# Position-bias stage: high parts of the weight split on ScalarE, low parts and refilling loads one chunk later, three buffers for the mirrored copies

## Chip, core and metric

One Trainium2 chip, one core. The metric is the device time of one execution in microseconds (us), median of three runs. Engine names are those of the profile: PE is TensorE (PEld its weight loads), DVE is VectorE, ACT is ScalarE, POOL is GpSimd, SP is the engine that issues most DMAs ("SPq" rows).

## What is computed

Attention with a learned position bias, a gated dense layer, and a routed mixture of experts:

```python
psi_rel = np.log1p(np.abs(pos[:, None] - pos[None, :]))
x = (psi_rel / psi_i)[..., None]
bias = np.maximum(x @ w1 + b1, 0.0) @ w2            # one bias matrix per head, 576 x 576
scores = q @ k.T / np.sqrt(D) + bias                # 4 batches, 8 heads
x = softmax(scores) @ v                             # 2304 tokens x 512
x = ((x @ m_w1) * (x @ m_w2) @ w3) @ w_out          # dense layer
out = routed_experts(x)                             # 8 experts, one per token
```

The dense layer's last two matrices are multiplied with each other ahead of time (w3 times w_out). That product, and the position bias, are the work of the first stage of the kernel, the function `p0`. The change touches this stage alone.

## The kernel before

**Two jobs in one stage.** `p0` runs two jobs side by side. The first builds the position bias in nine groups (gg = 0 to 8) of 3 to 5 row tiles t. For each group 16 masks are made, nine on ACT and seven on DVE (line 262 on DVE, line 260 on ACT). For each tile of a group PE runs 48 small matmuls on the masks (line 341) into one of three PSUM buffers `pb`; `evac` then scales one half on ACT (line 267, `tmp`) and adds both halves on DVE (line 278, `ds`). A tile's evacuation is written one tile later than its matmuls. After every second group `flush` sends each `ds` tile to DRAM (`dsym`, line 220), and where the tile has a mirrored half POOL copies it in reverse, four heads at a time, into a buffer `md` (line 234), which a DMA writes to `dsym` too (line 237). There are two `md` buffers; a copy waits until the DMA of the copy two before it has read its buffer.

**The second job.** w_out and w3 arrive as raw 64-bit numbers in 24 chunks c of 128 x 512 (8 of w_out, then 16 of w3, two for each block f), over five raw buffers. A chunk is converted to float32 by one ACT step (line 88, done a whole chunk ahead by `begin`) and three DVE steps (lines 90, 91, 92). It is then split for TensorE: the high part is a rounded copy (line 201, on POOL), the low part is the difference of the number and its high part (line 206, on DVE). Where the low part is written, the refilling load of the chunk five further on is put into SP's queue (line 179). When both parts are there, `wp_mm` multiplies (line 244, three matmuls for each of 64 steps, 48 of them in this stage and 16 in the next); after eight steps ACT copies the result into a buffer of the same `md` ring (line 248) and SP sends it off (line 249, `wp`).

**The order.** Engines take their instructions in the order in which the program writes them. Within a tile that order is: the `wp_mm` steps that `WPH` gives to the tile, the tile's 48 matmuls, the ACT half of the previous tile's evacuation, two or three ACT masks, a slice of the list `mixed`, the DVE half of the evacuation with its flush, and the tasks of `ahead` (from group 3 on: the loads of q, k and v of the first head at the second tile of group 3, and from the fourth tile on the steps that split them, the first of which is an ACT copy of q, line 402). `mixed` holds the DVE masks of the next group, the placing of the coefficients (line 160), and the conversion steps, sorted by a due time between 0 and 1. A group converts `CONV[gg+1] - CONV[gg]` chunks. For chunk number x of a group of n chunks the three DVE steps are due at (x + 0.125)/n, (x + 0.375)/n and (x + 0.625)/n, the high part at (x + 0.75)/n, and the low part with the load at (x + 1.25)/n but at the end of the group at the latest. For the last chunk of every group, so, the low part stands right behind the high part.

POOL's other work in this stage is the mirrored copies, the coefficients of a later group (lines 151, 153, 165) and some of the steps that split q, k and v.

Of the kernel before, what the change touches and what calls it, by code (L numbers as in the profile page):

```python
# [9 lines left out]
F32 = mybir.dt.float32  # L10
# [5 lines left out]
ALU = mybir.AluOpType  # L16
# [4 lines left out]
B, H, S, D = 4, 8, 576, 64  # L21
HID = 32
NT = B * S
DM = 512
FF = 1024
E = 8
P = 128
# [15 lines left out]

CV = [(i, b) for i in range(12) for b in range(2)]
CONV = (0, 5, 9, 11, 13, 16, 17, 20, 22, 24)
WPH = (0, 0, 0, 2, 12, 16, 31, 32, 43, 48)

NACT = 9

FM = 0.6  # L50
NRAW = 5


LAG = 6
# [15 lines left out]
class Kern:  # L70
# [4 lines left out]
    def T(self, pool, shape, dt, tag, **k):  # L75
        self.n += 1
        return pool.tile(shape, dt, name=f"{tag}_{self.n}", tag=tag, **k)
# [18 lines left out]
    def p0(self, dsym, wp_dram, late, ahead=lambda gg, ti: None):  # L96


        nc, tc, I, T = self.nc, self.tc, self.I, self.T
        with ExitStack() as es:  # L100
# [3 lines left out]
            st = es.enter_context(tc.tile_pool(name="p0s", bufs=2, side="right"))  # L104
# [37 lines left out]
            gp = nc.gpsimd  # L142
# [32 lines left out]
            def load(i, b):  # L175
                raws[i, b] = T(st, [P, DM, 2], I32, "w3", bufs=NRAW)
                src = I["w_out"][:, 2 * i:2 * i + 2, :] if i < 4 else I["w3t"][i - 4]
                src = src.rearrange("p k d -> p (k d)")[:, DM * b:DM * b + DM]
                nc.sync.dma_start(out=raws[i, b].rearrange("p n t -> p (n t)"), in_=src.bitcast(I32))
# [3 lines left out]
            def begin(n):  # L183
                if n < len(CV):
                    i, b = CV[n]
                    t_, steps = self.conv_steps(st, raws.pop((i, b)), "w3t", bufs=4)
                    steps[0]()
                    begun[i, b] = t_, steps[1:]

            def conv(i, b):  # L190

                t_, steps = begun.pop((i, b))
                if i < 4:
                    hi, lo = (w[:, 2 * i + b, :] for w in (woh, wol))
                else:
                    if b == 0:
                        w3hl[i - 4] = [T(late.wp, [P, KF, P], F32R, n, bufs=2) for n in ("w3h", "w3l")]
                    hi, lo = (w.rearrange("p k f -> p (k f)")[:, DM * b:DM * b + DM] for w in w3hl[i - 4])

                def part():  # L200
                    gp.tensor_scalar(out=hi, in0=t_, scalar1=1.0, scalar2=1.0, op0=ALU.mult, op1=ALU.mult)

                def rest():
                    if order:
                        load(*order.pop(0))
                    v.tensor_tensor(out=lo, in0=t_, in1=hi.bitcast(F32), op=ALU.subtract)

                return steps + [part, rest]
# [3 lines left out]
            def flush(t, kk, d):  # L212
                n = 64 if t == 4 else P
                w = min(128, DMAX[t] - 128 * kk)
                sg = -1 if t >= 2 else 1
                if sg > 0:
                    c0 = OFF[t] + 128 * kk
                else:
                    c0 = OFF[t] - 128 * kk - w + 1
                nc.sync.dma_start(out=dsym[:, t, 0:n, c0:c0 + w].rearrange("h p w -> p h w"), in_=d[:n, :, 0:w])  # L220
                other = OFF[t] if t < 2 else 702 - OFF[t]
                m = min(128 * kk + w - 1, other)
                d0 = max(128 * kk, 1)
                if m < d0:
                    return
                if sg > 0:
                    c1, c2 = OFF[t] - m, OFF[t] - d0 + 1
                    l1 = w - 1 - (m - 128 * kk)
                else:
                    c1, c2 = OFF[t] + d0, OFF[t] + m + 1  # L230
                    l1 = d0 - 128 * kk
                for h in range(0, H, 4):
                    md = T(st, [P, 4, 128], F32, "md")
                    gp.tensor_scalar(
                        out=md[:n, :, 0:w], in0=bass.AP(d.tensor, d.offset + 128 * h + w - 1, [[d.ap[0][0], n], [128, 4], [-1, w]]),
                        scalar1=1.0, scalar2=1.0, op0=ALU.mult, op1=ALU.mult)
                    nc.sync.dma_start(out=dsym[h:h + 4, t, 0:n, c1:c2].rearrange("h p w -> p h w"), in_=md[:n, :, l1:l1 + c2 - c1])

            def wp_mm(f, k, pools=(ps1, st)):
                if k == 0:  # L240
                    pws[f] = T(pools[0], [P, DM], F32, "pv")
                hi, lo = w3hl[f]
                for j, (a, b_) in enumerate(((hi, woh), (hi, wol), (lo, woh))):
                    nc.tensor.matmul(out=pws[f], lhsT=a[:, k, :], rhs=b_[:, k, :],  # L244
                                     start=(k == 0 and j == 0), stop=(k == KF - 1 and j == 2))
                if k == KF - 1:
                    wsb = T(pools[1], [P, DM], F32, "md") if pools[1] is st else T(pools[1], [P, S], F32, "t")[:, 0:DM]
                    nc.scalar.copy(out=wsb, in_=pws.pop(f))
                    nc.sync.dma_start(out=wp_dram[:, f, :], in_=wsb)

# [32 lines left out]
            order = list(CV)  # L283
            for _ in range(NRAW):
                load(*order.pop(0))
# [10 lines left out]
                    pl()  # L296
            pl = coefs(1)
            prev = None
            for gg in range(9):
                ts = [t for t in (0, 4, 3, 1, 2) if 64 * gg < DMAX[t]]  # L300
                wph = list(range(WPH[gg], WPH[gg + 1]))
                bg, bga = [], []
                if gg < 8:
                    for q in range(16):
                        act = (q + 1) * NACT // 16 > q * NACT // 16
                        (bga if act else bg).append(lambda q=q, act=act: mask(gg + 1, q, act))

                cs = []
                n = CONV[gg + 1] - CONV[gg]
                for x, (i, b) in enumerate(CV[CONV[gg]:CONV[gg + 1]]):  # L310

                    cs += [((x + (k + 0.5) / 4) / n, (i, b, k)) for k in range(3)]
                    cs += [((x + 0.75) / n, (i, b, 3)), (min((x + 1.25) / n, 1), (i, b, 4))]
                st_ = {}

                def cstep(i, b, k):
                    if k == 0:
                        begin(CV.index((i, b)) + 1)
                        st_[i, b] = conv(i, b)
                    st_[i, b][k]()  # L320

                items = [(FM * (k + 0.5) / len(bg), x) for k, x in enumerate(bg)]
                items += [(k, lambda x=x: cstep(*x)) for k, x in cs]
                if gg < 8:
                    items.append((0, pl))
                    if gg == 0:
                        items.append((0, lambda: place(1, 1, c3)))
                    if gg < 7:
                        pl = coefs(gg + 2)
                mixed = [x for _, x in sorted(items, key=lambda x: x[0])]  # L330
                nt = len(ts)
                for ti, t in enumerate(ts):
                    for x in wph[len(wph) * ti // nt:len(wph) * (ti + 1) // nt]:
                        wp_mm(x // KF, x % KF)
                    n = 64 if t == 4 else P
                    pb = T(ps, [P, 2, 2, H, 8, 4], F32, "pb")
                    mv = mvs[gg % 2]
                    for s in range(16):
                        m_ = mss[gg, s // 8]
                        for k in range(3):  # L340
                            nc.tensor.matmul(out=pb[:n, s // 8, :, :, s % 8], lhsT=m_[:, s % 8, P * t:P * t + n], rhs=mv[:, k, s], start=(k == 0), stop=(k == 2))  # L341
                    fin = evac(*prev) if prev else None
                    for x in bga[len(bga) * ti // (nt - 1):len(bga) * (ti + 1) // (nt - 1)]:
                        x()
                    m0, m1 = len(mixed) * ti // nt, len(mixed) * (ti + 1) // nt
                    for x in mixed[m0:m1]:
                        x()
                    if fin:
                        fin()
                    ahead(gg, ti)  # L350
                    prev = (gg, t, pb)
            evac(*prev)()
            return [lambda pools, x=x: wp_mm(x // KF, x % KF, pools) for x in range(WPH[9], KF * KF)]


# [1183 lines left out]
```

## Time and profile before

| | us |
|---|---|
| median of 3 runs (lowest, highest) | 1094.40 (1093.64, 1094.58) |
| the profiled execution | 1096.77 |
| span of its trace | 1094.9 |

The profiled execution's span is 1094.9 us, and 1.9 us lie around it; the execution itself was 2.4 us longer than the median. The stage `p0` takes the first 168 us of the span: its last `ds` row ends there and the score matmuls of the attention (line 480) begin. In the trace the groups begin, by their first row of line 160, at 37.2 (group 1), 57.7 (2), 76.3 (3), 97.4 (4), 119.9 (5), 134.8 (6) and 149.9 us (7).

A row of a timeline gives start and duration in us, then engine, line, operation, tiles, and in brackets how long the engine stood idle before it and what it waited for. The row of a wait gives the waiting engine and line, what it waited for, the sum in us, how many times, and the longest. Times in the prediction are us from the span's start.

### The profile page before, as it was taken

The page shows a single profiled execution, that of the slowest core. Times are in us where ns is not written, and L with a number is a line of the kernel's source. Part 1 is how long each engine was busy: PE and PEld are TensorE (multiplying, and loading weights), DVE is VectorE, ACT ScalarE, POOL GpSimd, SP SyncE. Part 2 cuts the span into 40 slices and gives each one's busy share as a digit, 9 for nine tenths or more (in the row PEclk, how much of TensorE's full clock was granted, in tenths as well). Part 3 has the DMA queues.
Part 4 walks back from the last instruction along what each step waited for, and adds up shares of the span by engine and source line. Part 5 has one row for each costly group of instructions (what it writes and reads, how often), then busy time and mean ns, then how long its engine had stood idle before and what let it go on. Part 6 is the DMA issues. An engine that isn't in the chain of part 4 may idle for free.

```text
span 1094.9 us, 21996 instructions
## 1 busy us (share of the span) xinstructions
PE 1009.9 (92%) x8118; PEld 903.7 (83%) x8118; DVE 795.1 (73%) x1490; ACT 668.2 (61%) x1248; POOL 403.5 (37%) x475
## 2 busy tenths in 40 slices
PE   3575887999999999989999999999979999999995
PEld 3565776888888888869999999999978888888884
DVE  8875997899999999999722212221478899989995
ACT  5555465888898988844322222222125888888884
POOL 3443625787888878544400000000043112111120
PEclk9788898999999999989999999999989999999998
DMA  4579677333534341234110000000233316411272
GB/s 133 144 211 227 170 202 206 120 113 109 166 114 131 103 148 56 65 125 141 63 39 1 20 20 20 11 11 20 95 108 111 129 49 212 171 40 39 67 252 94
DMA packets 62419, 116.54 MB, mean 106 GB/s; under 512 B 14495, under 2 KB 33567, under 8 KB 62048
## 3 DMA queue, kind: packets, MB, share of 16 engines
q1 hardware_dynamic: 58496, 104.14, 31.0%
q0 software_dynamic: 3520, 10.75, 2.9%
q8 instruction: 67, 1.10, 0.4%
q14 instruction: 48, 0.39, 0.1%
q10 hardware_dynamic: 288, 0.15, 0.1%
HBM read 155.68 MB, written 25.15 MB: 165 GB/s over the span
## 4 chain that ended last, share of the span: by engine, by line
PE 49%; issue 15%; DMA 11%; DVE 7%; ACT 1%; POOL 0%; POOLq 0%; DVEq 0%; ACTq 0%
PE ab L711 16%; DMA out<-or,sci 9%; PE sc L480 8%; PE o L780 8%; PE pv L566 6%; PE tr L517 5%; PE pv L561 3%; DMA raw<-in_w 2%; PE pv L510 1%; PE pv L244 1%; DVE cva L91 1%; DVE cva L90 1%; DVE cva L89 1%; DVE cva L92 1%; DVE su L501 0%
## 5 line engine op out<-in xcount | busy, mean ns | idle before, releaser
L506 POOL TENSOR_SCALAR e<-e,su 128x576 f32<-128x576 f32 x144 | 114.9, 801 | 58.7 <-DVE su L502 45.0
L757 DVE TENSOR_TENSOR g<-ab,asb 128x256 f32<-128x256 f32 x72 | 30.4, 422 | 143.3 <-ACT asb L756 143.0
L341 PE MATMUL pb<-mv,mask 128*128 128x64 bf16 (+1 forms) x1872 | 73.6, 206 | 53.0 <-DVE ds L278 40.1
L341 PEld LDWEIGHTS <-mask 128*128 128x128 bf16 (+1 forms) x1872 | 70.0, 111 | 61.1 <-issue 53.1
L487 DVE CUSTOM_DVE_ANT_0 t<-sc,nb 128x576 f32<-128x576 f32 x144 | 108.3, 752 | 14.8 <-PE sc L480 12.5
L496 ACT ACTIVATE e<-t,mn 128x576 f32<-128x576 f32 x144 | 112.2, 779 | 7.4 <-DVE mn L487 5.9
L547 DVE TENSOR_TENSOR etl<-tr,eth 128x512 fp32r<-128x512 f32 x144 | 98.5, 684 | 7.4 <-ACT eth L538 4.3
L480 PE MATMUL sc<-kh,qs 128*128 128x288 f32 x320 | 97.6, 322 | 4.9 <-DVE ds L278 4.9
L538 ACT CAST eth<-tr 128x512 fp32r<-128x512 f32 x144 | 83.7, 581 | 28.6 <-PE tr L517 26.2
L1327 POOL DMA_INDIRECT out<-or,sci x21 | 24.8, 1180 | 204.5 <-ACT or L1326 194.8
L1224 DVE TENSOR_TENSOR w1l<-w1r,w1h 128x1024 fp32r<-128x1024 f32 x80 | 92.6, 1220 | 5.0 <-ACT w1h L1223 5.0
L711 PE MATMUL ab<-xh,wh 128*128 128x256 f32 x576 | 94.8, 287 | 0.4 <-DVE g L757 0.4
L1275 DVE TENSOR_TENSOR w2l<-w2r,w2h 128x1024 fp32r<-128x1024 f32 x80 | 92.6, 1220 | 2.6
L711 PE MATMUL ab<-xh,wl 128*128 128x256 f32 x576 | 93.5, 285 | 0.3 <-POOL wl L676 0.3
L711 PE MATMUL ab<-xl,wh 128*128 128x256 f32 x576 | 93.4, 285 | 0.0
L952 POOL DMA_INDIRECT xh<-x2r,gi x1 | 1.4, 1350 | 243.8 <-DMA w1r<-in_w1e 243.8
L480 PE MATMUL sc<-kl,qs 128*128 128x288 f32 x320 | 89.8, 296 | 0.0
L517 PE MATMUL tr<-k_ident,e 128*128 128x128 f32 x576 | 86.5, 273 | 3.2 <-DVE etl L547 3.2
L480 PEld LDWEIGHTS sc<-kh,qs 128*128 128x128 f32 x320 | 60.6, 189 | 31.4 <-issue 11.6
L1223 ACT CAST w1h<-w1r 128x1024 fp32r<-128x1024 f32 x84 | 82.2, 1068 | 0.0
L711 PEld LDWEIGHTS ab<-xh,wh 128*128 128x128 f32 x576 | 80.0, 193 | 0.8 <-DVE g L757 0.6
L711 PEld LDWEIGHTS ab<-xh,wl 128*128 128x128 f32 x576 | 80.2, 193 | 0.5 <-POOL wl L676 0.5
(313 smaller groups left out, 2817.0 us busy)
## 6 DMA issues: line engine op xcount, KB each, us to landing
w1r<-in_w1e SPq DMA_DIRECT2D x84, 512.0 KB
w2r<-in_w2e SPq DMA_DIRECT2D x80, 512.0 KB
q<-in_qd SPq DMA_DIRECT2D x16, 576.0 KB
k<-in_kd SPq DMA_DIRECT2D x16, 576.0 KB
w<-in_w3t SPq DMA_DIRECT2D x16, 512.0 KB
raw<-in_w SPq DMA_DIRECT2D x16, 512.0 KB
nb<-dsym SPq DMA_DIRECT2D x7, 1152.0 KB
dsym<-ds SPq DMA_DIRECT2D x14, 512.0 KB
```

What stands on the lines that cost most here:

```text
L341: nc.tensor.matmul(out=pb[:n, s // 8, :, :, s % 8], lhsT=m_[:, s % 8, P * t:P * t + n], rhs=mv[:, k, s], start=(k == 0), stop=(k == 2))
L480: nc.tensor.matmul(out=sc[:, f, 0:288], lhsT=l, rhs=r, start=(n == 0), stop=(n == len(lst) - 1))
L487: nc.vector.tensor_tensor_reduce(out=t_.rearrange("p (f k) -> p f k", f=2), in0=sc[:, :, 0:288], in1=pre.nb[h % 2][:, tt, :].rearrange("p ...
L496: nc.scalar.activation(out=e, in_=t_, func=AF.Exp, scale=-1.0, bias=mn, accum_out=su[:, i % 2:i % 2 + 1])
L506: nc.gpsimd.tensor_scalar(out=e, in0=e, scalar1=su[:, i % 2:i % 2 + 1], scalar2=1.0, op0=ALU.mult, op1=ALU.mult)
L517: nc.tensor.transpose(pt[:, kb, :], e[:, P * kb:P * kb + P], ident)
L538: nc.scalar.copy(out=dh, in_=src)
L547: nc.vector.tensor_tensor(out=dl, in0=src, in1=dh.bitcast(F32), op=ALU.subtract)
L711: nc.tensor.matmul(out=p[:, a], lhsT=w[f][:, a, k, :], rhs=x[:, k, :], start=(k == 0 and n == 0), stop=(k == KD - 1 and n == 2))
L780: nc.tensor.matmul(out=o[:, a, 0:c1 - c0], lhsT=g[:, sl], rhs=w[:, f, c0:c1], start=(f == 0 and n == 0), stop=(f == KF - 1 and n == 2))
L1224: eng.tensor_tensor(out=w1l[:, k], in0=w1r[:, k], in1=w1h[:, k].bitcast(F32), op=ALU.subtract)
L1275: nc.vector.tensor_tensor(out=w2l[:, sl], in0=w2r[:, sl], in1=w2h[:, sl].bitcast(F32), op=ALU.subtract)
```

## The change

The high part of a chunk is copied by ACT in place of POOL (24 copies). The due times of the steps are new: the three DVE steps and the high part at 0.1, 0.3, 0.5 and 0.7 of a chunk, and at 0.9 the low part and the refilling load of the chunk before, across the borders of groups. The very last chunk's low part comes at the end of group 8. The ring of the mirrored copies, `md`, has three buffers in place of two. `WPH` gives the product steps to other groups: groups 2 to 6 had 2, 10, 4, 15 and 1 of them, now 0, 8, 8, 12 and 4.

```diff
-WPH = (0, 0, 0, 2, 12, 16, 31, 32, 43, 48)
+WPH = (0, 0, 0, 0, 8, 16, 28, 32, 43, 48)
+NMD = 3
...
                 def part():
-                    gp.tensor_scalar(out=hi, in0=t_, scalar1=1.0, scalar2=1.0, op0=ALU.mult, op1=ALU.mult)
+                    nc.scalar.copy(out=hi, in_=t_)
...
-                    md = T(st, [P, 4, 128], F32, "md")
+                    md = T(st, [P, 4, 128], F32, "md", bufs=NMD)
...
-                    wsb = T(pools[1], [P, DM], F32, "md") if pools[1] is st else T(pools[1], [P, S], F32, "t")[:, 0:DM]
+                    wsb = T(pools[1], [P, DM], F32, "md", bufs=NMD) if pools[1] is st else T(pools[1], [P, S], F32, "t")[:, 0:DM]
...
+            st_ = {}
             for gg in range(9):
...
-                for x, (i, b) in enumerate(CV[CONV[gg]:CONV[gg + 1]]):
-
-                    cs += [((x + (k + 0.5) / 4) / n, (i, b, k)) for k in range(3)]
-                    cs += [((x + 0.75) / n, (i, b, 3)), (min((x + 1.25) / n, 1), (i, b, 4))]
-                st_ = {}
-
-                def cstep(i, b, k):
+                for x, c_ in enumerate(range(CONV[gg], CONV[gg + 1])):
+
+                    cs += [((x + 0.1 + 0.2 * k) / n, (c_, k)) for k in range(4)]
+                    if c_:
+                        cs.append(((x + 0.9) / n, (c_ - 1, 4)))
+                if gg == 8:
+                    cs.append((1, (len(CV) - 1, 4)))
+
+                def cstep(n, k):
                     if k == 0:
-                        begin(CV.index((i, b)) + 1)
-                        st_[i, b] = conv(i, b)
-                    st_[i, b][k]()
+                        begin(n + 1)
+                        st_[n] = conv(*CV[n])
+                    st_[n][k]()
```

## Rows read from the trace of the kernel before

**Rows 1.** The page, parts 1 and 2: engines over the span; 40 slices, in tenths.
```profile
PE 1009.9 (92%) x8118; PEld 903.7 (83%) x8118; DVE 795.1 (73%) x1490; ACT 668.2 (61%) x1248; POOL 403.5 (37%) x475
DVE  8875997899999999999722212221478899989995
DMA  4579677333534341234110000000233316411272
```
**Rows 2.** Busy time by stretch: stretch, its length, engines (x instructions), granted clock, DMA share, GB/s.
```profile
0.00:168.00 168.00, 110.08 (x2017) 96.68 (x2017) 134.65 (x252) 92.65 (x150) 70.34 (x118) 0.87 0.68 182
45.00:73.00 28.00, 17.86 (x352) 16.12 (x350) 19.27 (x37) 14.65 (x24) 12.21 (x20) 0.79 0.90 223
76.00:97.00 21.00, 14.04 (x266) 11.75 (x265) 12.24 (x24) 11.35 (x18) 6.97 (x10) 0.91 0.74 206
97.00:120.00 23.00, 15.86 (x259) 13.76 (x258) 17.94 (x29) 11.45 (x18) 12.89 (x19) 0.77 0.85 195
150.00:168.00 18.00, 13.10 (x222) 10.89 (x220) 16.25 (x33) 7.39 (x14) 3.66 (x5) 0.94 0.79 222
```
**Rows 3.** Waits of DVE from 0 to 168 us.
```profile
DVE w3l L206 <- POOL w3h L201: 24.3, 10, 8.7
DVE xT L206 <- POOL xT L201: 3.6, 4, 1.8
DVE mv L160 <- PE pb L341: 0.9, 1, 0.9
```
**Rows 4.** Waits of POOL (first 180 us) and ACT (first 168 us).
```profile
POOL md L234 <- DMA dsym<-md: 16.2, 6, 5.5
POOL md L234 <- ACT mask L260: 8.0, 1, 8.0
ACT md L248 <- DMA dsym<-md: 6.0, 2, 3.8
ACT qs L402 <- DMA q<-in_qd: 4.9, 1, 4.9
```
**Rows 5.** Timeline around DVE's longest wait, group 3, in order of time.
```profile
84.53 0.46 SPq L386 DMA_DIRECT2D q<-in_qd  x1
86.03 1.17 SPq L249 DMA_DIRECT2D wp<-md  x1
86.48 0.99 DVE L92 SCALAR_TENSOR_TENSOR w3ta<-w,w3ta 128x512 int32<-128x512 int32 x1
91.29 0.67 ACT L402 CAST qs<-q 128x576 fp32r<-128x576 f32 x1 [4.90 <-DMA q<-in_qd]
91.87 1.26 ACT L267 ACTIVATE tmp<-pb,ivb 128x512 f32<-128x512 f32 x2
94.97 0.62 POOL L234 TENSOR_SCALAR md<-ds 128x512 f32<-128x512 f32 x1 [8.04 <-ACT mask L260]
95.55 0.62 POOL L201 TENSOR_SCALAR w3h<-w3ta 128x512 fp32r<-128x512 f32 x1
96.20 0.69 DVE L206 TENSOR_TENSOR w3l<-w3ta,w3h 128x512 fp32r<-128x512 f32 x1 [8.73 <-POOL w3h L201]
```
**Rows 6.** Groups of instructions by line and shape, 0 to 168 us.
```profile
L248 ACT COPY md<-pv 128x512 f32<-128x512 f32 x6 | 3.5, 586 | 15.4 <-PE pv L244 7.1 <-DMA dsym<-md 6.0 <-POOL qs L1409 2.3
L201 POOL TENSOR_SCALAR w3h<-w3ta 128x512 fp32r<-128x512 f32 x16 | 10.3, 644 | 33.7 <-DVE w3ta L92 33.7
L206 DVE TENSOR_TENSOR w3l<-w3ta,w3h 128x512 fp32r<-128x512 f32 x16 | 12.7, 794 | 24.3 <-POOL w3h L201 24.3
```
**Rows 7.** Timeline of PE: one tile's matmuls, and the stage's last ones.
```profile
80.52 1.57 PE L341 MATMUL pb<-mv,mask 128*128 128x64 bf16 x48
97.55 2.72 PE L341 MATMUL pb<-mv,mask 128*64 128x64 bf16 x48 [7.51 <-DVE ds L278]
161.31 1.71 PE L341 MATMUL pb<-mv,mask 128*64 128x64 bf16 x48
167.91 0.61 PE L480 MATMUL sc<-kh,qs 128*128 128x288 f32 x1 [4.90 <-DVE ds L278]
```

## The prediction

> **What bounds the kernel now.** I read the page first: over the whole span PE is the busy engine, but in the first six of 40 slices, 27 us each, DVE stands at 5 to 9 tenths (it reads 8 8 7 5 9 9) [rows 1]. These slices are the stage that the change touches, and the rest of the kernel is taken as fixed. Next come the stretches: of the stage's 168 us DVE works 134.7, PE 110.1, ACT 92.7, POOL 70.3, and the DMA engines are 0.68 busy [rows 2]. DVE has the most work, so the question is what its 33 idle us are. The waits answer it: 27.9 us (24.3 + 3.6, in 14 waits) are low parts that wait for POOL's high part; the only other wait inside the stage's run is 0.9 us on PE [rows 3], and the rest is the start.
>
> Why is POOL late with a copy of 0.64 us [rows 6]? POOL's own waits show it: it stands 16.2 us for a mirrored buffer whose DMA has not read it, and 8.0 us more under the name of an ACT mask [rows 4]. The timeline shows what that last one is. POOL waits until 94.97 with a mirrored copy; of the two `md` buffers one is held by the product block that SP sent off at 86.03, behind the loads of q, k and v (q alone, issued at 84.53, released ACT at 91.29). So a DMA is the releaser that fits. The high part stands behind that mirrored copy in POOL's order (95.55), and DVE, done with its last step at 87.47 (86.48 + 0.99), gets its high part at 96.2: 8.7 us [rows 5]. PE in turn waits 7.5 us for DVE to free a PSUM buffer [rows 7]. The path is DMA, mirrored buffer, POOL, DVE.
>
> **The change part by part.** *High parts to ACT.* The 14 waits name one producer, and it leaves their path: 27.9 us come off DVE. A low part now comes a chunk after its high part, so that even the short waits, where the low part stood right behind the high part, are covered by the next chunk's three DVE steps. In group 8 the last two low parts stand together; the first, 0.69 us [rows 5], covers the last ACT copy. The copy on ACT is bounded by 0.586 us (its copy of 512 columns from PSUM) and 0.67 us (its copy of 576 columns from SBUF) [rows 5, 6]; I take 0.6, near the first, since the columns agree: 24 x 0.6 = 14.4 us. ACT goes from 92.7 to 107 us in a stage that would then last some 150; it hides, and I cost it at nothing. Without that cover it is 14.4 us. The copy makes ACT wait for DVE's last step of the same chunk. Behind it on ACT stand the next tile's `tmp` and masks; `tmp` is needed only at the end of the next tile's DVE slice, so this wait is covered too. POOL loses 24 copies of some 0.65 us, on an engine that is off the path.
>
> *What is late next: ACT's copy of q.* In group 3 ACT waits 4.90 us for q's DMA [rows 4]. Today that hides under POOL's 8.7 us. After the change DVE does not wait for the high part (it is ahead of the q copy on ACT), writes its low part by 88.1 and then needs the evacuation's `tmp`, which ACT starts at 91.87 and ends some 0.65 later, at 92.5: 4.4 us. `WPH` puts the last step of block 0 into this very tile, so a copy of 0.59 us stands ahead of `tmp`: 5.0 us. I take 4.7. It shifts with the stage, as q's issue hangs on the same DVE progress; bounds 3 (q lands a little sooner) and 8 (q queued behind a backlog of flushes).
>
> *The three buffers and the DMA.* With three buffers the tile that stuck at 94.97 finds a free one, the more so as block 0's product copy now comes after it. But the DMA work itself stays. From 45 to 120 us it is 0.90 x 28 + 0.74 x 21 + 0.85 x 23 = 60 us, and some 2 in the three us between; DVE works 19.3 + 12.2 + 17.9 = 49.4 there, some 52 with the gap [rows 2]. With the 4.7 us of q that is 57 against 62. So in these groups DVE can no longer run free: bias tiles are reused after two groups, once the flush has read them, and the loads queue behind flushes. What is over can slide into the lighter time after 120 us (the fifth slice has 6 tenths [rows 1]), so I charge 3 of the 5 us; bounds 0 and 8.
>
> *Loads one chunk later.* In SP's queue each load now stands behind up to one more tile's flush, and SP waits there for POOL's mirrored copies; behind it stand later loads and flushes. Five raw buffers still leave about two chunks of lead, where three were. In the trace of before ACT's DMA waits are for q and for mirrored buffers [rows 4], none for a raw load; I cost it at nothing beyond the 3 us above, bounds 0 and 3 us for each of ten loads (below).
>
> *Product steps moved.* Their total stays 48. Group 3 loses two of ten, groups 4 and 6 gain four and three, group 5 loses three. PE has 14.0 us of work in group 3 [rows 2], and DVE will leave it about 17. A tile takes PE 1.57 us at full clock and 2.72 at the slow one after idling [rows 7]; should group 3 begin slow, PE is late by some us. I take 1.5, bounds 0 and 4. At the end of the stage PE is done at 163.0 and waits 4.9 us for DVE [rows 7], so the three us that DVE gains after 130 are not eaten by PE.
>
> *Ports.* The low part's row is 0.794 us in the mean, against 0.69 for the one at 96.20 [rows 5, 6]: 16 x 0.10 = 1.7 us that may come back if POOL's copies cause it; I count none. The Trainium skill ("SBUF — State Buffer", section "SBUF: two separate sides") says that GpSimd and a VectorE instruction with two SBUF inputs lock each other out of a shared pair of ports, while ScalarE has its own; by that the 1.7 us would come off too and the sum below would be 20.4. This trace has the longer mean, but does not tell which POOL work made it.
>
> **The sum.** 27.9 - 4.7 - 3 - 1.5 = 18.7 us. The profiled execution's 1096.8 (span 1094.9 and 1.9 around it) would become 1078.1, its span 1076.2; the median lies 2.4 below that execution, so 1094.4 - 18.7 = 1075.7, which I give as 1076. The stage would end at 168 - 18.7 = 149.
>
> **The rivals.**
> *A, DMA takes the place of POOL.* The stretch from 45 to 120 cannot be shorter than its DMA work, 62 us, and none slides out: 75 - 62 = 13 us come off there instead of the 22.6 us of idle DVE in those three stretches [rows 2]. Outside it 27.9 - 22.6 = 5 us are left to gain; half of q's wait still shows (2.4), PE takes 1.5: 14 us, and with transfers not packed without gaps 12, so 1082. For it: shares of 0.85 and 0.90. Against: a share over a stretch need not be a limit, and buffers let it lag.
> *B, late loads stop ACT, slower.* ACT now carries the high parts, the masks, the evacuation and the conversion's first step in one order; a raw load that has not landed stops them all. Ten loads are queued in groups 1 to 4, among flushes. The gain without them, 27.9 - 6.2 (q and PE) = 21.7, is gone when each costs 2.2 us; at 3 us each, under half of q's 6.8 from issue to use [rows 5], it is 30 + 6.2 - 27.9 = 8 us slower: 1103. Against: two chunks of lead, 6 us and more. The Trainium skill ("DMA: Bandwidth & Descriptors", section "Rules for kernel authors") advises to issue a transfer early and wait for it late; the moved loads go against that, and its sentence gives no size. No row here shows the lead running out.
> *C, all covers hold.* Only 3 us of q are left: 25 us off, 1069.
> *D, no effect.* Another engine paces the stage at the same length: 1094. Hardly, with PE at 110 of 168.
>
> **Chances.** Forecast 0.68, A 0.18, C 0.07, B 0.05, D 0.02. The forecast's own bounds are 27.9 - 3 = 25 and 27.9 - 8 - 8 - 4 = 8 us off, 1069 to 1086; with a little beyond C the range is 1067 to 1086, which leaves out B, D and the ends of the others. Faster by over 0.2% (about what a measurement of this kernel can tell from no change) 0.93, within 0.2% 0.02, slower 0.05.
>
> **What would show it.** Right: no DVE wait for a high part, ACT's copies of some 0.6 us, the stage's end near 149, DVE's longest wait about 5 us in group 3 and on ACT's `tmp`, POOL's wait for mirrored buffers smaller or harmless. Rival A: DVE waiting for bias tiles or ACT for buffers while the DMA share stays over 0.9 from 45 on. Rival B: ACT conversions (line 88) waiting for loads. The prediction is wrong if DVE's idle time in the stage stays above 20 us, or if the attention behind it begins slower than before.

## The result and the profile after

The changed kernel runs at 1076.4 us (1075.6 to 1077.2, four runs) beside 1094.4 of the kernel before: a ratio of 0.984, 95% interval 0.982 to 0.985, or 18.0 us less. The forecast was 1076. The profiled execution's span is 1074.9 us, 20.0 shorter than that of before.

In the changed file lines are shifted: the conversion steps stand in lines 89 and 91 to 93, `place` in 161, the high part in 202, the low part in 207, the mirrored copy in 235, the product copy in 249, masks in 261 and 263, `tmp` and `ds` in 268 and 279, ACT's copy of q in 406.

The page of the changed kernel, the same lines as [rows 1]:

```profile
PE 1006.9 (94%) x8118; PEld 900.3 (84%) x8118; DVE 795.3 (74%) x1490; ACT 680.1 (63%) x1272; POOL 393.2 (37%) x451
DVE  8998978999999999999512221223487999899994
DMA  4599983343334322144000000000323326311272
```

ACT has 24 instructions more and 12 us more work, POOL 24 fewer. DVE's work is what it was, but the dip in its fourth slice, 5 tenths in [rows 1], is 8 now, and the DMA engines stand at 9 9 9 8 from the third to the sixth slice.

The stretches of the changed kernel, columns as in [rows 2]; the stage's last `ds` row now ends at 147.4 us (167.9 before):

```profile
0.00:149.00 149.00, 107.64 (x2021) 93.86 (x2022) 134.62 (x253) 104.57 (x174) 60.14 (x94) 0.91 0.78 206
45.00:73.00 28.00, 21.14 (x448) 19.46 (x448) 26.84 (x46) 22.56 (x36) 16.17 (x22) 0.83 0.95 232
```

DVE works 134.6 us in both kernels, in 149 instead of 168. From 45 to 73 us it worked 19.3 of 28 before [rows 2] and 26.8 now. What is left of the kernel takes 927.5 us after the stage's end (927.0 before), so the whole gain lies in the stage.

The waits of the changed kernel in its first 150 us, where [rows 3] and [rows 4] had those of before:

```profile
POOL md L235 <- DMA dsym<-md: 20.3, 5, 12.2
DVE ds L279 <- ACT tmp L268: 4.6, 2, 3.8
ACT qs L406 <- DMA q<-in_qd: 4.6, 1, 4.6
ACT w3ta L89 <- DMA w<-in_w3t: 4.5, 2, 4.0
DVE ds L279 <- DMA dsym<-ds: 2.7, 2, 1.6
DVE ds L279 <- POOL p3a L152: 0.9, 1, 0.9
```

No low part waits for a high part any more. POOL still stands 20.3 us for mirrored buffers, 12.2 of them at once, and no row of DVE names such a copy. The last row names another POOL instruction, and the timeline shows what its 0.9 us are:

```profile
97.71 0.59 ACT L249 COPY md<-pv 128x512 f32<-128x512 f32 x1 [2.22 <-POOL p3a L152]
98.19 0.69 ACT L268 ACTIVATE tmp<-pb,ivb 128x512 f32<-128x512 f32 x1
98.97 0.69 DVE L279 TENSOR_TENSOR ds<-pb,tmp 128x512 f32<-128x512 f32 x1 [0.91 <-POOL p3a L152]
```

DVE goes on right behind `tmp` (98.19 + 0.69 = 98.88), and ahead of `tmp` ACT's product copy of block 1 had waited 2.2 us for a buffer of the ring. In the program's order that buffer held a mirrored copy that POOL had finished before 93 us, so its DMA is the releaser that fits. DVE's waits inside the run are 4.6 + 2.7 + 0.9 = 8.2 us; they were 27.9 + 0.9 = 28.8 [rows 3]. The difference, 20.6 us, is the 20.5 by which the stage ends earlier.

The timeline of group 3, where [rows 5] had DVE's longest wait:

```profile
78.61 1.09 DVE L207 TENSOR_TENSOR w3l<-w3ta,w3h 128x512 fp32r<-128x512 f32 x1
81.72 0.67 ACT L406 CAST qs<-q 128x576 fp32r<-128x576 f32 x1 [4.55 <-DMA q<-in_qd]
82.29 0.58 ACT L249 COPY md<-pv 128x512 f32<-128x512 f32 x1
82.77 0.69 ACT L268 ACTIVATE tmp<-pb,ivb 128x512 f32<-128x512 f32 x1
83.50 0.69 DVE L279 TENSOR_TENSOR ds<-pb,tmp 128x512 f32<-128x512 f32 x1 [3.79 <-ACT tmp L268]
```

It is the chain that the prediction named: q's DMA, ACT's copy of q, the product copy, `tmp`, DVE. DVE waits 3.8 us behind it.

### The profile page after: what moved, and what is told of

It reads as the page before. It is cut to its first block, busy times and chain, and to the rows that moved or that the text cites. A ratio compares the mean times of both kernels' runs of the same rounds, so it can differ in the third digit from the quotient of the medians.

```text
span 1074.9 us, 21998 instructions
## 1 busy us (share of the span) xinstructions
PE 1006.9 (94%) x8118; PEld 900.3 (84%) x8118; DVE 795.3 (74%) x1490; ACT 680.1 (63%) x1272; POOL 393.2 (37%) x451
## 4 chain that ended last, share of the span: by engine, by line
PE 50%; issue 17%; DMA 14%; DVE 14%; ACT 3%; POOL 0%; SPq 0%; POOLq 0%; DVEq 0%; ACTq 0%
PE ab L715 16%; DMA out<-or,sci 10%; PE sc L484 8%; PE o L784 8%; PE pv L570 6%; PE tr L521 5%; PE pv L565 3%; DMA dsym<-ds 2%; DVE mv L161 2%; DVE mask L263 2%; DVE ds L279 1%; DMA dsym<-md 1%; DMA raw<-in_w 1%; PE pv L514 1%; PE pv L245 1%
## 5 line engine op out<-in xcount | busy, mean ns | idle before, releaser
L715 PE MATMUL ab<-xl,wh 128*128 128x256 f32 x576 | 92.9, 284 | 0.0
L484 PEld LDWEIGHTS sc<-kh,qs 128*128 128x128 f32 x320 | 60.8, 190 | 30.9 <-issue 16.1
```

The source lines that it names most:

```text
L484: nc.tensor.matmul(out=sc[:, f, 0:288], lhsT=l, rhs=r, start=(n == 0), stop=(n == len(lst) - 1))
L715: nc.tensor.matmul(out=p[:, a], lhsT=w[f][:, a, k, :], rhs=x[:, k, :], start=(k == 0 and n == 0), stop=(k == KD - 1 and n == 2))
```

## Experiments

The parts are tested alone and in pairs first. "Order" is the new due times, the later loads and the new `WPH` together; a gain is against the kernel before on the same chip. The last column is read from each kernel's trace, one execution: where the stage ends (its last `ds` row), how much of that time DVE works, and how long it stands idle.

| high part on | order | mirrored buffers | median us | gain us | ratio, 95% interval | stage's end: DVE works + idle, us |
|---|---|---|---|---|---|---|
| POOL | old | 2 | 1094.4 | | | 167.9: 134.7 + 33.2 |
| ACT | old | 2 | 1083.1 | 11.2 | 0.990 (0.9885 to 0.992) | 155.3: 129.9 + 25.4 |
| POOL | old | 3 | 1091.5 | 2.8 | 0.998 (0.997 to 0.999) | 164.0: 135.8 + 28.2 |
| POOL | new | 2 | 1090.9 | 3.4 | 0.997 (0.996 to 0.998) | 163.2: 139.1 + 24.2 |
| ACT | new | 2 | 1087.7 | 6.6 | 0.994 (0.992 to 0.996) | 159.2: 136.2 + 22.9 |
| POOL | new | 3 | 1086.3 | 9.3 | 0.991 (0.988 to 0.994) | 157.5: 137.7 + 19.9 |
| ACT | new | 3 | 1076.4 | 18.0 | 0.984 (0.982 to 0.985) | 147.4: 134.5 + 12.9 |

ACT with the old order and three buffers was not tried. The new order gains 3.4 and 6.5 us with the high parts on POOL and loses 4.6 with ACT and two buffers, so whether the changed kernel needs it beside the other two parts is not shown.

DVE has the same 252 instructions in every row of the table, and still its work differs by up to 9 us. Why is told under "The ports" below.

### The high parts on ACT, alone

```diff
 # the kernel before
-                    gp.tensor_scalar(out=hi, in0=t_, scalar1=1.0, scalar2=1.0, op0=ALU.mult, op1=ALU.mult)
+                    nc.scalar.copy(out=hi, in_=t_)
```

> One part alone, on the kernel before: the high part is copied by ACT; the order of the steps, WPH and the two mirrored buffers are old. Theory (POOL, stuck behind mirrored copies, was what held DVE): the three long waits (8.7, 5.8, 4.3 us) shrink to about 5, 0 and 0; but each low part that stands right behind its high part still waits for ACT, 0.6 us and more where ACT is at masks, some ten times. Gain 27.9 - 5 - 8 - 2 for the DMA = 13 us: 1081 (1077 to 1085). Rival 1 (the new order is what counts, the engine hardly): gain under 5 us, over 1089. Rival 2 (the engine is everything): 1077 or less.

Measured: 1083.1, inside the range, 11.2 us gained for the expected 13. DVE's and ACT's longest waits in this kernel:

```profile
85.59 0.69 DVE L206 TENSOR_TENSOR w3l<-w3ta,w3h 128x512 fp32r<-128x512 f32 x1 [4.88 <-ACT w3h L201]
106.23 0.59 ACT L248 COPY md<-pv 128x512 f32<-128x512 f32 x1 [7.08 <-DMA dsym<-md]
107.94 0.69 DVE L206 TENSOR_TENSOR w3l<-w3ta,w3h 128x512 fp32r<-128x512 f32 x1 [7.52 <-ACT w3h L201]
```

The first is the wait for q, as expected. The second was not: ACT's product copy takes its buffer from the same ring as the mirrored copies, waits 7.1 us for one of their DMAs, and holds the high part behind it. The DMA wait that stopped POOL now stops ACT. Neither rival holds: the engine alone brings over half, not all. Waits are not all of it: of the 12.6 us by which the stage ends earlier, 7.9 are idle time of DVE, and 4.7 are its own rows, which take 129.9 us in place of 134.7.

### Three mirrored buffers, alone

```diff
 # the kernel before
-                    md = T(st, [P, 4, 128], F32, "md")
+                    md = T(st, [P, 4, 128], F32, "md", bufs=3)      # the product copy's too
```

> One part alone, on the kernel before: three mirrored buffers; POOL keeps the high parts, the order is old. Theory: POOL is stuck for less, so that of the 18.8 us of long waits half goes, part of it given back to the wait for q; the eleven short waits (9.1 us) stay. Gain about 7 us: 1087 (1083 to 1091). Rival (the DMA work itself paces groups 1 to 4, the number of buffers does not): gain under 2 us, over 1092.

Measured: 1091.5, a gain of 2.8 us for the expected 7; a miss, nearer to the rival. DVE's waits in groups 3 and 4:

```profile
90.28 0.69 DVE L278 TENSOR_TENSOR ds<-pb,tmp 128x512 f32<-128x512 f32 x1 [2.40 <-ACT tmp L267]
106.16 0.69 DVE L206 TENSOR_TENSOR w3l<-w3ta,w3h 128x512 fp32r<-128x512 f32 x1 [8.92 <-POOL w3h L201]
```

The 8.7 us of [rows 5] became 2.4 behind q, and the wait appears again a group later with 8.9 us. A third buffer moves the point at which POOL is stuck; the high part still stands behind it.

### The new order, alone

```diff
 # the changed kernel
-                    nc.scalar.copy(out=hi, in_=t_)
+                    gp.tensor_scalar(out=hi, in0=t_, scalar1=1.0, scalar2=1.0, op0=ALU.mult, op1=ALU.mult)
-NMD = 3
+NMD = 2
```

> One part alone: the new order (due times, low part and load one chunk later, WPH), with the high parts on POOL and two mirrored buffers as before. Theory: a low part now follows its high part by a chunk, 3 to 4 us, which covers all eleven short waits (9.1 us) and some 3.5 us of each long one; what is left is POOL stuck for 8.0, 5.5 and 3 us. Gain 27.9 - 4.5 - 2 - 5 (q) - 2 = 14 us: 1080 (1075 to 1086). Rival (only the engine matters): gain under 3 us, over 1091.

Measured: 1090.9, a gain of 3.4 us for the expected 14; the rival's mechanism is not the reason either:

```profile
96.09 0.59 ACT L249 COPY md<-pv 128x512 f32<-128x512 f32 x1 [7.82 <-DMA dsym<-md]
97.30 0.69 DVE L279 TENSOR_TENSOR ds<-pb,tmp 128x512 f32<-128x512 f32 x1 [12.09 <-ACT tmp L268]
```

The short waits for the high part are gone as expected. But the new `WPH` puts the first product copy behind two mirrored copies and into the tile after ACT's wait for q. With two buffers it waits 7.8 us, on top of q's 5, and `tmp` and DVE wait with it. DVE idles 9.0 us less than before, but its own rows take 4.4 us more.

### The changed kernel with two buffers

```diff
 # the changed kernel
-NMD = 3
+NMD = 2
```

> The changed kernel with two mirrored buffers in place of three. Theory: with the high parts on ACT, POOL's stalls no longer hold DVE; but SP waits for POOL's copies with the loads behind it, and ACT's product copies use the same ring. The cost is 1 to 4 us: 1079 (1077 to 1081). Rival (the buffers are the main gain): 1083 and more. Other rival (buffers idle once ACT has the high parts): 1076 to 1077.

Measured: 1087.7, 11 us slower than the changed kernel where 1 to 4 were expected. The rival that calls the buffers the main gain has the size right. The timeline of group 3:

```profile
82.96 0.67 ACT L406 CAST qs<-q 128x576 fp32r<-128x576 f32 x1 [5.14 <-DMA q<-in_qd]
91.69 0.58 ACT L249 COPY md<-pv 128x512 f32<-128x512 f32 x1 [8.06 <-DMA dsym<-md]
92.90 0.69 DVE L279 TENSOR_TENSOR ds<-pb,tmp 128x512 f32<-128x512 f32 x1 [11.85 <-ACT tmp L268]
```

One DVE wait of 11.9 us, where the changed kernel has 3.8. Here the third buffer keeps the moved product copy from making ACT wait; whether it serves POOL too is asked further below. The wait does not tell why ACT with the new order and two buffers (6.6 us) gains less than ACT alone (11.2). In all, DVE idles less here than there; its own rows take longer. The stage with ACT alone, then this one (columns as in [rows 2]):

```profile
0.00:155.27 155.27, 107.62 (x2016) 94.07 (x2016) 129.91 (x252) 105.04 (x174) 59.49 (x94) 0.88 0.72 197
0.00:159.15 159.15, 107.53 (x2016) 93.20 (x2016) 136.23 (x252) 104.69 (x174) 58.29 (x94) 0.89 0.71 191
```

DVE works 129.9 us there and 136.2 here, in 252 instructions each, and idles 25.4 and 22.9.

### The changed kernel with the high parts on POOL

```diff
 # the changed kernel
-                    nc.scalar.copy(out=hi, in_=t_)
+                    gp.tensor_scalar(out=hi, in0=t_, scalar1=1.0, scalar2=1.0, op0=ALU.mult, op1=ALU.mult)
```

> The changed kernel with the high parts back on POOL (new order and three mirrored buffers kept). Theory: the lag of one chunk covers the short waits, three buffers shorten POOL's stalls, but after's trace has POOL stuck 12.2 us in group 3 and 4.5 us in group 2 with mirrored copies, and a high part behind those would come too late by some 8 and 1 us, of which the q wait (3.8 us) already hides part. 5 to 6 us slower than the changed kernel: 1082 (1079 to 1086). Rival (the lag alone covers everything, ACT adds nothing): 1077 and less.

Measured: 1086.3 with a before of 1095.5, 9.3 us gained, so 8.7 less than the changed kernel for the expected 5 to 6; nothing speaks for the lag alone. DVE's two long waits on POOL:

```profile
69.93 1.08 DVE L207 TENSOR_TENSOR w3l<-w3ta,w3h 128x512 fp32r<-128x512 f32 x1 [3.43 <-POOL w3h L202]
103.67 0.69 DVE L207 TENSOR_TENSOR w3l<-w3ta,w3h 128x512 fp32r<-128x512 f32 x1 [4.50 <-POOL w3h L202]
```

A lag of a chunk covers the short waits, and these two remain, after stalls on mirrored buffers: the mechanism is that of [rows 5], at half the length. It is not the whole cost. The stage of this kernel, then of the changed one:

```profile
0.00:157.54 157.54, 108.61 (x2016) 95.31 (x2016) 137.67 (x252) 92.46 (x150) 82.31 (x118) 0.87 0.73 193
0.00:147.37 147.37, 106.16 (x2016) 92.39 (x2016) 134.48 (x252) 104.57 (x174) 60.14 (x94) 0.92 0.78 207
```

Of the 10.2 us by which the stage ends later, 7.0 are idle time of DVE and 3.2 are its own rows. The expectation had the waits near that and the rows at nothing.

### ACT's copy of q later

```diff
 # the changed kernel
-        tasks = [first, lambda: None] + ...
+        tasks = [first, lambda: None, lambda: None, lambda: None] + ...
```

> The changed kernel with ACT's copy of q (and all steps that split q, k and v) two tiles later; the loads stay where they are. It measures the term that the prediction puts at 4.7 us and the trace of after at 3.8 us (DVE waiting for tmp behind ACT's wait of 4.55 us for q). Theory: ACT does not wait, DVE's 3.8 us go, and 1 to 2 of them come back as waits for the flush, as the DMA work is the same: 1073.5 (1072 to 1075.5). Rival A of the prediction (DMA paces groups 1 to 4): the time moves to the next DMA wait, 1076 to 1077.

Measured: 1078.1 with a before of 1095.5, ratio 0.984 (0.982 to 0.986), the same as the changed kernel. The wait for q is gone, and a group later stands another:

```profile
97.99 0.59 ACT L249 COPY md<-pv 128x512 f32<-128x512 f32 x1 [6.48 <-POOL md L235]
99.25 0.69 DVE L279 TENSOR_TENSOR ds<-pb,tmp 128x512 f32<-128x512 f32 x1 [5.00 <-ACT tmp L268]
```

From the first `place` row of group 3 to that of group 5 it takes 32.5 us (67.3 to 99.9), and 32.7 (66.8 to 99.6) in the changed kernel: group 3 is 4.5 us shorter, group 4 is 4.3 longer. The row of the copy names POOL, but it is the place of the 2.2 us in the changed kernel, with the same holder of the buffer: POOL had finished that mirrored copy by 92.9, so its DMA fits. The 3.8 us behind q were not a cost of their own; what DVE gains there it loses to the next buffer that a DMA holds. The rival is right.

### The loads of q, k and v early

Two forms: the whole first task in group 0, and only its loads (1.5 MB and two small ones), with POOL's two memsets left in group 3.

```diff
 # the changed kernel; first form: first() at gg == 0 and ti == 1
         def ahead(gg, ti):
+            if gg == 0 and ti == 3:
+                for n in ("ident", "wg"):
+                    nc.sync.dma_start(out=cst[n], in_=I[n])
+                pre.load(0)
...
-            pre.load(0)     # in first(), as the two small loads
```

> The changed kernel with the loads of the first q, k and v (1.5 MB, and two small ones) in group 0, where the DMA share is low, in place of group 3. ACT's wait for q goes as in the run with q later, and 1.5 MB leave the time in which the DMA engines are nearly full. Theory (DVE bound, DMA waits small): 3.8 us plus most of the other DMA-caused waits (0.85 + 0.91 + 1.03): 1071 (1069.5 to 1073.5). Rival A (DMA paces): this run gains clearly more than the run with q later, by 3 us or more. If both gain the same, DMA work does not matter there.

> The changed kernel with only the loads of the first q, k and v (and two small ones) moved to group 0, fourth tile; the two memsets of POOL stay in group 3. In the run with q early these memsets stood ahead of coefficients on POOL and the loads beside the first constants, and group 1 began 2 us later. Theory (DMA work of 1.5 MB taken out of groups 3 and 4 is worth 4 us of the stretch from group 3 to group 5, which measured 28.3 us against 32.7): 1071 (1069 to 1073), of which DVE's wait behind q is 3.8. Rival (the gain of the run with q early is only the q wait, and group 2 loses to the flush what is gained): 1073 to 1075.

Measured: 1074.5 with a before of 1095.5, ratio 0.980 (0.9775 to 0.983), and 1074.6 with a before of 1095.8, ratio 0.980 (0.978 to 0.982). Each gains 21 us on the kernel before, 3 more than the changed kernel (0.4% by the ratios; only the second form's interval lies clear of the changed kernel's). The first form was measured beside the same runs of before as the kernel with q's copy later: it is 3.6 us faster, and its slowest run is faster than that kernel's fastest. The second form's stretch from group 3 to group 5 is 29.4 us (68.3 to 97.8), 3.3 less than in the changed kernel. So the same ACT wait, taken away with its DMA work, pays, and taken away without it does not. The waits of DVE that remain in the second form, and the rows behind the second of them:

```profile
DVE ds L279 <- DMA dsym<-ds: 5.2, 2, 2.9
DVE ds L279 <- POOL md L235: 1.7, 1, 1.7
95.90 0.59 ACT L249 COPY md<-pv 128x512 f32<-128x512 f32 x1 [2.98 <-POOL resta L154]
96.38 0.69 ACT L268 ACTIVATE tmp<-pb,ivb 128x512 f32<-128x512 f32 x1
97.16 0.69 DVE L279 TENSOR_TENSOR ds<-pb,tmp 128x512 f32<-128x512 f32 x1 [1.68 <-POOL md L235]
```

The first is the flush: bias tiles that are not yet read out. The second is `tmp` again, behind the product copy of block 1, which waits 3.0 us for the ring. The expected 1071 was not reached; the time is the one that the rival gave, and group 2's wait for the flush grew from 1.0 to 2.9 us, as the rival said.

### Loads one chunk sooner

```diff
 # the changed kernel
                 def part():
                     nc.scalar.copy(out=hi, in_=t_)
+                    if order:
+                        load(*order.pop(0))
 
                 def rest():
-                    if order:
-                        load(*order.pop(0))
```

> The changed kernel with the refilling load put into SP's queue at the high part of its own chunk, not with the low part a chunk later. It undoes that part of the change alone. Theory: late loads cost what ACT waits for raw loads in the trace of after, 4.0 us once, of which 0.85 reaches DVE: 0 to 1.5 us faster, 1075.5 (1074.5 to 1077). Rival B of the prediction (late loads stop ACT): 3 us faster or more.

Measured: 1077.2 with a before of 1095.5, ratio 0.982 (0.980 to 0.9845): no difference from the changed kernel that can be told. ACT waits for no raw load any more, and DVE's other waits are longer instead:

```profile
DVE ds L279 <- DMA dsym<-ds: 4.9, 2, 2.8
DVE ds L279 <- POOL md L235: 3.3, 1, 3.3
101.31 0.58 ACT L249 COPY md<-pv 128x512 f32<-128x512 f32 x1 [4.36 <-POOL p3a L152]
```

The first is the flush (2.7 in the changed kernel). The second is again the product copy of block 1: it waits 4.4 us, and DVE goes on right behind its `tmp` (102.48). Late loads are not what slows this kernel, and rival B has no ground.

### More loads, and a buffer of its own

```diff
 # the changed kernel, in first(), behind the loads of q, k and v
+            for r in range(2):
+                nc.sync.dma_start(out=pre.nb[0][:, 2 * r:2 * r + 2, :], in_=I["qd"][1, :, 2 * r:2 * r + 2, :])
```

> The changed kernel with two loads more, 576 KB each, right behind the loads of q, k and v in group 3, into a tile that nobody reads before it is loaded again (the first head's bias); all else as it was. It doubles the suspected cost: DMA work in groups 3 and 4. Rival A of the prediction (DMA paces these groups): 1.15 MB at the 250 GB/s of the saturated stretch are 4.7 us, 3 to 5 us slower: 1080 (1079 to 1082). DVE-bound: the loads go by the side, 0 to 1 us: 1076 to 1077.5.

Measured: 1079.0 with a before of 1095.8, ratio 0.9845 (0.983 to 0.986). Against the changed kernel that is 0.9 us more by the ratios, and the two intervals overlap; the times do not decide. The trace points to a cost: the stage ends at 152.2 us, 4.8 later, and the span is 2.8 longer. One trace is weak evidence for it, as the kernel with the sooner loads ended its stage 3.7 us later in its trace and took the same time. The wait that grew, in group 4:

```profile
102.61 0.59 ACT L249 COPY md<-pv 128x512 f32<-128x512 f32 x1 [5.47 <-DMA dsym<-md]
103.87 0.69 DVE L279 TENSOR_TENSOR ds<-pb,tmp 128x512 f32<-128x512 f32 x1 [4.18 <-ACT tmp L268]
```

So DMA work added in group 3 comes out as a buffer wait in group 4, at the same product copy; how much of it reaches the end beside the changed kernel stays open between 1 and 3 us. A wider step does decide: the kernel with only the loads early was measured beside the same runs of before, issues 2.7 MB less of loads in group 3 than this one, and is 4.4 us faster; its slowest run is faster than this one's fastest.

```diff
 # the changed kernel
-NMD = 3
+NMD = 2
-wsb = T(pools[1], [P, DM], F32, "md", bufs=NMD) if ...
+wsb = T(pools[1], [P, DM], F32, "wsb", bufs=1) if ...
```

> The changed kernel with the same three buffers split: two for the mirrored copies, one for ACT's product copies alone. It tells what the third buffer does, which was worth 11 us where I had expected 1 to 4. Theory 1 (it keeps ACT's product copy of block 0, which stands ahead of tmp and of the high parts, from waiting for a mirrored copy's DMA; POOL's own stalls are harmless now): ACT's wait of 8.1 us in the kernel with two buffers goes, and so 1076 (1074 to 1079). Theory 2 (POOL's mirrored copies and SP's queue behind them are what counts): as slow as with two buffers, 1084 to 1088.

Measured: 1081.5 with a before of 1095.8, ratio 0.987 (0.986 to 0.989), between the two theories: 13.9 us gained on the kernel before (two shared buffers 6.6, three 18.0). The product copy's 8.1 us are gone, so a good half of the third buffer's worth is theory 1. Two waits of ACT stand where the rest went:

```profile
110.81 0.66 ACT L89 ACTIVATE w3ta<-w 128x512 f32<-128x512 f32 x1 [7.70 <-DMA w<-in_w3t]
147.61 0.59 ACT L249 COPY wsb<-pv 128x512 f32<-128x512 f32 x1 [3.17 <-DMA wp<-wsb]
```

SP stands longer before POOL's copies (26.7 us between 40 and 150, 19.6 in the changed kernel), which fits the first: ACT waits 7.7 us for a raw load that stands behind them in SP's queue (4.0 in the changed kernel). The second says that one product buffer is too few at the stage's end; DVE waits 3.2 us behind it. So the third buffer seems to serve POOL's copies too, through SP; how much of the 4.1 us that are missing goes to each wait is not shown.

A last kernel joined the early loads with three mirrored buffers and a product buffer of its own, with three instead of four buffers for converted chunks to make room:

```diff
 # the changed kernel, with the second form of the early loads
-t_, steps = self.conv_steps(st, raws.pop((i, b)), "w3t", bufs=4)
+t_, steps = self.conv_steps(st, raws.pop((i, b)), "w3t", bufs=3)
-wsb = T(pools[1], [P, DM], F32, "md", bufs=NMD) if ...
+wsb = T(pools[1], [P, DM], F32, "wsb", bufs=1) if ...
```

> The changed kernel with the loads of the first q, k and v in group 0 (as in the run with only the loads early), three mirrored buffers, a buffer of its own for ACT's product copies, and three in place of four buffers for converted chunks to make room. Theory: both waits of group 3 go, for q and for the shared buffers: 1 to 2 us faster than the run with the loads early, 1070 (1067.5 to 1072.5). Rival (fewer converted buffers make ACT wait for DVE's low parts): slower than that run.

Measured: 1074.5 with a before of 1095.8, ratio 0.980 (0.979 to 0.982), the same as with the early loads alone. In its trace ACT waits 5.0 us for the single product buffer near the stage's end, and DVE with it; group 7 began 1.8 us sooner than with the early loads alone, and that goes there.

## Why the prediction was right

**The removed wait** was read rightly: 28.8 us of waits on POOL and PE are gone from DVE. That the copy's engine alone takes them away was not right. With ACT alone, DVE still waits 18.1 us for high parts, now on ACT; in the changed kernel the lag of a chunk covers the short waits and the third buffer keeps ACT's product copy out of the way. With both in place, putting the copy back on POOL costs 8.7 us and brings back 8.4 us of waits for it.

**ACT's copies** were put at 0.6 us and cost 0.618 us each. Groups by line of the changed kernel in the stage:

```profile
L202 ACT CAST w3h<-w3ta 128x512 fp32r<-128x512 f32 x16 | 9.9, 618 | 10.6 <-DVE w3ta L93 8.1 <-PE pv L245 2.4
L207 DVE TENSOR_TENSOR w3l<-w3ta,w3h 128x512 fp32r<-128x512 f32 x16 | 11.8, 735 | 0.1
L161 DVE TENSOR_TENSOR mv<-p3a,bkb 128x512 bf16<-128x512 bf16 x27 | 21.4, 845 | 0.0
```

ACT is busy 104.6 us in 149, and none of DVE's waits names them: they hide.

**The terms of the sum**: behind q 3.8 us for 4.7; the DMA 4.4 us (2.7 for the flush, 0.9 behind the ring's buffer, 0.85 for a late load through `tmp`) for 3; PE none, and its old 0.9 gone, for 1.5. Together 8.2 of new waits for 9.2, and 20.6 us off the stage for 18.7. By the medians it is 18.0: the profiled execution of before was 2.4 us longer than its median, that of the changed kernel (1077.0) 0.6 longer than its own, and this difference of 1.8 lies between the two results. That 1076 and 1076.4 agree to half a us is luck: terms that are off by 0.9, 1.4 and 2.4 us cancel in part, and so does the difference between the two executions.

**What was right by its sum and not by its reasons.** The prediction treated the parts as a list of costs that add up. They do not. The third buffer got no price of its own; it is worth 11 us with the other two parts and 2.8 alone. The timelines give a reason: the product copy always shared the ring, but the new `WPH` lets block 0's take its buffer behind two mirrored copies (82.29 in the changed kernel) instead of ahead of them (80.76 in the kernel before); no run changed `WPH` by itself. And the 4.7 us behind q were taken for a cost that would go with its cause; moving the copy alone gave nothing back. The prediction had read the cause, 62 us of DMA work against 57 on DVE between 45 and 120 us, and had rival A for it. A's sign did show: the DMA share from 45 to 120 us is 0.93 in the changed kernel (0.90, 0.74 and 0.85 in the three stretches of [rows 2]). The runs put the truth between the forecast and A: DVE's waits in groups 3 and 4 are places where the same DMA lag shows. The third buffer and less DMA work there shorten them; moving the wait or the refilling loads does not.

**Rival B** (late loads) was tested and falls: ACT did wait 4.0 us for a load in group 5, 0.85 of which reached DVE, and sooner loads bring no time. Rivals C and D are out by the time.

**The ports.** The prediction counted nothing for DVE's own rows, and their sum is the same in both kernels, 134.7 and 134.5 us. This too is luck. In the three pairs of the table that differ by the copy's engine alone, ACT takes 2.8 to 4.7 us off DVE's rows; in the three that differ by the order alone, the new order adds 1.9 to 6.3. The two nearly cancel. The rows tell what stretches them. In the stages of all 14 traces, low parts of w3 with no POOL instruction beside them last 0.68 us (104 rows, none over 0.70); with one beside them they last 0.83 in the mean and up to 1.78 (120 rows). The `ds` rows, which read one of their two tensors from PSUM, last 0.68 either way (243 and 177 rows). Measured against like rows with POOL idle, POOL's work stretches DVE's rows in the stage by 16.6 us before, 11.8 with ACT alone, and 16.1 in the changed kernel. There the high-part copies are gone, but the mirrored copies stretch DVE by 4.5 us where it was 2.6. Why the new order brings DVE's rows beside more of POOL's work was not tested.

The low part's mean fell from 0.794 [rows 6] to 0.735 us, 0.9 us in 16 rows: 5 rows stood beside POOL before, at 1.04 us each, and 9 do now, at 0.78. The Trainium skill's rule, by which the prediction would have taken off 1.7 us ("SBUF — State Buffer", "SBUF: two separate sides"), fits in its kind; how much comes back depends on all of POOL's work and not on the copies alone. Other rows grew, such as line 161, from 18.5 to 21.4 us in 27 instructions.

## What to carry to other kernels

When a producer is moved to another engine, follow every instruction that stands ahead of it there, and each buffer that those take: a ring shared by two engines carries the old wait across. Before a wait is priced as a cost of its own, ask what feeds it; if it is DMA lag, test it both ways, once by moving the wait and once by moving the transfer. Compare the busy time of the engine that bounds the stage too, at the same count of instructions: another engine's work beside it can stretch it. And a total that comes out right does not confirm its terms; pairs of parts do.

## What was not expected of the hardware

One row of the changed kernel is more than twice as long as its like. The timeline of DVE and POOL at the start of group 5:

```profile
99.58 4.51 DVE L161 TENSOR_TENSOR mv<-p3a,bkb 128x512 bf16<-128x512 bf16 x3
99.98 1.72 POOL L410 TENSOR_TENSOR qs<-q,qs 64x576 fp32r<-64x576 f32 x1
101.78 1.76 POOL L413 TENSOR_TENSOR kl<-k,kh 128x576 fp32r<-128x576 f32 x1
```

These three DVE instructions take 1.88 us at 84.10, with POOL idle, and 4.51 here, beside two POOL subtractions of two tensors each; the 2.6 us more are below the 3.5 that POOL worked. In the kernel before, POOL's subtractions do not stand beside the same three at the start of group 5, but shorter coefficient steps do, and they take 2.21 us (at 119.93). Over the stages of the 14 traces, such a row lasts 0.68 us with POOL idle (191 rows, none over 0.70) and up to 1.91 beside POOL's work (187 rows). That fits the rule of the Trainium skill named above, that the two engines lock each other out for whole instructions.
